# Root of the lead tiles by logarithm and exponential on ScalarE, first weight columns between the x tiles, parameter transposes behind the first tile

## Chip, cores and metric

One NeuronCore of a Trainium2 chip runs the whole kernel. The metric is device time in microseconds (us) of one execution; the kernel before took 180.91 us, the median of three runs (180.74 to 181.76). The engines are named as in the profile: PE is TensorE (PEld its weight loads), DVE is VectorE, ACT is ScalarE, POOL is GpSimd, and SP is SyncE, whose queue issues nearly all transfers.

## What is computed

The input x has 2048 tokens of 512 values. A layer normalization without weights feeds two branches, which are added to x: a diagonal state-space model with complex states (512 states, run over the 2048 tokens), and a gated feed-forward network with 1376 hidden columns.

```python
xn = (x - mean(x)) / sqrt(var(x) + 1e-5)             # over the 512 values of a token
dt = exp(log_dt); Lam_bar = exp(dt * (Lambda_re + 1j * Lambda_im))
Bu = xn @ (((Lam_bar - 1) / Lam)[:, None] * B).T     # complex
h[t] = Lam_bar * h[t - 1] + Bu[t]                    # the scan over tokens
y_A = 2 * real(h @ C.T) + xn * Dskip
y_B = (gelu(xn @ w_gate) * (xn @ w_up)) @ w_down
out = x + y_A + y_B
```

Inputs, weights and output are bf16.

## The kernel before

**Tiling.** The 2048 tokens are 16 tiles of 128, in four blocks of four tiles. For each block TensorE makes `Bu` (L671), the gate and up projections in 11 slices of up to 128 hidden columns (`gu_mm`, L728), and the down projection with the output of the state-space model added into the same PSUM bank (L802, L813). VectorE rotates and scans the states (`CHAIN`), multiplies gelu by up and evicts the output; ScalarE evicts PSUM (L680, L736, L738), applies gelu, and normalizes blocks 2 and 3.

**How the order is made.** The kernel records operations with the buffers that they read and write, and a planner with assumed durations (`Sched`) orders them. TensorE and SP keep the order of the program text. On VectorE, ScalarE and GpSimd the planner chooses, except that operations handed to `S.pin(...)` stand first, in exactly that order. `emit` (L241) then writes each operation with the semaphore waits ahead of it. An engine does its queue strictly in order, so an operation that waits holds up whatever is queued behind it. Where an activation needs a function that isn't in the table that ScalarE holds, the build puts an `ACT_TABLE_LOAD` directly in front of the activation, behind any wait that stands as an instruction of its own. Before has four of them: ahead of the first exponential (L609), the first gelu (L838), the sine (L622) and the next gelu (L838).

**The lead.** This is the stretch until TensorE begins `BU(0)` at L671, and all edits lie in it. The four tiles of block 0 are normalized one at a time so that TensorE can start early. For lead tile tt:

- `stats` (L522): VectorE takes mean and variance (L524, L525).
- `rsqrt` (L543): GpSimd adds epsilon (L544) and raises to the power -0.5 (L545).
- `center` (L537): VectorE subtracts the mean and multiplies by the root (L540). `LN_lead` (L547) pins the order on VectorE: the statistics of two tiles, centring 0, statistics 2, centring 1, statistics 3, centring 2, centring 3.
- `TR_lead` (L555): TensorE transposes the tile in four matmuls (L562) into a PSUM bank, and ScalarE copies it into `XNT` (L565, "evT").
- `lead_mm` (L833): TensorE multiplies the transposed tile by two slices each of gate and up, 8 matmuls of 128 columns for a pair of slices (L728). The program text orders them tile by tile, with the transposes between.

Ahead of and between these stand matmuls on zeros (`warm_pe`, L825), whose results nobody reads.

**The parameters.** Three vectors of 512 (log_dt, Lambda_re, Lambda_im) come as 4x128 and are turned by three small transposes on TensorE (`TR_par`, L572). ScalarE makes `exp_dt` (L609), four `exp_a` (L611) and two copies (L614, L615) from them, and VectorE the angles (L616 to L621) and the tables of sine and cosine (L626 to L630, ScalarE L632 and L633).

**SP's queue.** It issues, in this order: x tiles 0 to 3, the first 256 columns of gate and of up (`ld_gu(0)`), two transposing loads of B, then further columns and x tiles. ScalarE's queue issues the three parameter loads.

Of the kernel before, what the change touches and what calls it, by code (L numbers as in the profile page):

```python
# [10 lines left out]
ACTF = mybir.ActivationFunctionType  # L11
BF16, F32, I32 = dt.bfloat16, dt.float32, dt.int32
# [297 lines left out]
EPS_LN = 1.0e-5  # L310
# [13 lines left out]
def d_act(n, ptr=0): return 100.0 + 0.833 * n + 90.0 * ptr  # L324


def build(nc, ins, out):
    with ExitStack() as es:
        E = es.enter_context
        S = Sched(nc, es)  # L330
        ARENA_BYTES = 207 * 1024
        arena_t = E(nc.sbuf_tensor("arena", [128, ARENA_BYTES // 2], BF16))
        A = Arena(arena_t, ARENA_BYTES)
# [10 lines left out]
        WG = A.alloc("WG", [KD, F + 32], BF16)  # L344
        WU = A.alloc("WU", [KD, F], BF16)
        WD = A.alloc("WD", [KF, D], BF16)
        FCH = [(0, 256), (256, 640), (640, 1024), (1024, F)]
        WGc = [Buf("WGc%d" % i, "wg", i, i + 1) for i in range(len(FCH))]
        WUc = [Buf("WUc%d" % i, "wu", i, i + 1) for i in range(len(FCH))]
# [39 lines left out]
        MVt = [[A.sub(MV[b], "MV%d_%d" % (b, j), j) for j in range(4)] for b in range(NB)]  # L389

        def per_tile(name, dtype=F32):
            al = A.alloc(name, [NB, 4], dtype)
            blk = ring(al, name, NB)
            return blk, [[A.sub(blk[b], "%s%d_%d" % (name, b, j), j) for j in range(4)] for b in range(NB)]
        RQb, RQt = per_tile("RQ")
        NRQb, _ = per_tile("NRQ")
        NHALF = A.alloc("NHALF", [4], F32)
        HPI = A.alloc("HPI", [1], F32)
        DUM = A.alloc("DUM", [2], F32)
        LRE = A.alloc("LRE", [KP], BF16)  # L400
# [45 lines left out]
        def V(fn, dur, r, w, tag="", after=(), slack=0.0):  # L446
            op = S.op("vector", fn, dur, r, w, tag, after)
            op.slack = slack
            return op

        def ACT(fn, dur, r, w, tag="", after=(), slack=0.0):
            op = S.op("scalar", fn, dur, r, w, tag, after)
            op.slack = slack
            return op
        POOL = lambda fn, dur, r, w, tag="": S.op("gpsimd", fn, dur, r, w, tag)
        PE = lambda fn, dur, r, w, tag="": S.op("tensor", fn, dur, r, w, tag)

        def load(dst, src, nbytes, writes, tag, queue="sync"):
            return S.dma(lambda e: e.dma_start(dst, src), nbytes, writes=writes, tag=tag, queue=queue)  # L459

        def ld_x(t0, n, queue="sync"):
            return load(X_all.ap[:, t0:t0 + n, :], x2[128 * t0:128 * (t0 + n), :].rearrange("(j p) d -> p j d", p=128),
                        n * 128 * 1024, X[t0:t0 + n], "ld_x", queue)

        def ld_w(W, Wc, src, ci, queue="sync"):
            f0, f1 = FCH[ci]
            return load(W.ap[:, :, f0:f1], src[:, f0:f1].rearrange("(k p) f -> p k f", p=128),
                        512 * (f1 - f0) * 2, [Wc[ci]], "ld_w", queue)

        def ld_param(T_, nm, queue="sync"):  # L470
            return S.dma(lambda e: e.dma_start(T_.ap[0:KP, :], ins[nm].rearrange("(s p) -> s p", p=128)), 1024,
                         writes=[T_], tag="ld_" + nm, queue=queue, lat=2300.0)

        def ld_tr(dst, nm):
            return S.dma(lambda e: e.dma_start_transpose(dst.ap, ins[nm]), 4.0 * 1000 * 330, writes=[dst], tag="tr_" + nm,
                         issue=1900.0, lat=1000.0)

        def ld_gu(ci):
            ld_w(WG, WGc, ins["B_w_gate"], ci)
            ld_w(WU, WUc, ins["B_w_up"], ci)  # L480

        S.pin(*[ld_param(T_, nm, "scalar") for T_, nm in ((PRM[0], "A_log_dt"), (PRM[1], "A_Lambda_re"), (PRM[2], "A_Lambda_im"))])
        for tt in range(4):
            ld_x(tt, 1)
        ld_gu(0)
        ld_tr(BBT[0], "A_B_re")
        ld_tr(BBT[1], "A_B_im")
        ld_gu(1)
# [5 lines left out]
        def late_loads():  # L494
# [6 lines left out]
            ld_x(12, 4)  # L501

        POOL(lambda e: e.memset(NHALF.ap, -0.5), 100, [], [NHALF], "const")
        POOL(lambda e: e.iota(IOT.ap, [[1, 128]], base=0, channel_multiplier=-1), 300, [], [IOT], "iota")
        POOL(lambda e: e.iota(IOTJ.ap, [[1, 512]], base=0, channel_multiplier=0), 600, [], [IOTJ], "iotj")
        ZWs = [Buf("ZWa", "sb", ZW.lo, ZW.lo + 256, ZW.ap[:, 0:128]), Buf("ZWb", "sb", ZW.lo + 256, ZW.hi, ZW.ap[:, 128:512])]
        S.pin(V(lambda e: e.memset(ZWs[0].ap, 0.0), 100, [], ZWs[0:1], "zw"),
              V(lambda e: e.memset(ZWs[1].ap, 0.0), 200, [], ZWs[1:2], "zw"),
              V(lambda e: e.memset(HPI.ap, 0.5 * math.pi), D_TINY, [], [HPI], "hpi"),
              V(lambda e: e.memset(DUM.ap, 0.0), D_TINY, [], [DUM], "dum"),  # L510
# [11 lines left out]
        def stats(tt):  # L522
            b, j = divmod(tt, 4)
            return [V(lambda e: e.bn_stats(ST[tt].ap, X[tt].ap), 640, [X[tt]], [ST[tt]], "bnst", slack=4000.0),  # L524
                    V(lambda e: e.bn_aggr(MVt[b][j].ap, ST[tt].ap), 100, [ST[tt]], [MVt[b][j]], "bnag", slack=4000.0)]  # L525
# [11 lines left out]
        def center(tt):  # L537
            b, j = divmod(tt, 4)
            m = MVt[b][j]
            return V(lambda e: e.tensor_scalar(XN[tt].ap, X[tt].ap, m.ap[:, 0:1], RQt[b][j].ap, ALU.subtract, ALU.mult),  # L540
                     d_dve_ts4x(512) + 40, [X[tt], m, RQt[b][j]], [XN[tt]], "ln", slack=2500.0 if b == 1 else 0.0)

        def rsqrt(dst, var, r, n):  # L543
            POOL(lambda e: e.tensor_scalar(dst.ap, var, EPS_LN, None, ALU.add), 250, r, [dst], "eps")  # L544
            POOL(lambda e: e.tensor_tensor(dst.ap, dst.ap, NHALF.ap[:, 0:n], ALU.pow), (400 + 250 * n) * (1 if n == 1 else 2.5), [dst, NHALF], [dst], "pow")  # L545

        def LN_lead():  # L547
            st = [stats(tt) for tt in range(4)]
            ln = []
            for tt in range(4):  # L550
                rsqrt(RQt[0][tt], MVt[0][tt].ap[:, 1:2], [MVt[0][tt]], 1)
                ln.append(center(tt))
            S.pin(*st[0], *st[1], ln[0], *st[2], ln[1], *st[3], ln[2], ln[3])

        def TR_lead(tt):  # L555
            bank = 6 + tt % 2
            pt = PSH[bank][:, 0:512]

            def f(e):
                ins_ = None  # L560
                for dk in range(KD):
                    ins_ = e.transpose(pt[:, 128 * dk:128 * dk + 128], XN[tt].ap[:, 128 * dk:128 * (dk + 1)], IDN.ap)  # L562
                return ins_
            PE(f, 400, [XN[tt], IDN], [BANK[bank]], "T0")
            return ACT(lambda e: e.activation(XNT[0].ap[:, :, 128 * tt:128 * tt + 128],  # L565
                                              pt.rearrange("p (k t) -> p k t", k=KD), ACTF.Copy),
                       d_act(512), [BANK[bank]], [XNTt[tt]], "evT")
# [4 lines left out]
        def TR_par(i):  # L572
            PE(lambda e: e.transpose(PP[i], PRM[i].ap[0:KP, :], IDN.ap[0:KP, 0:KP]), 100, [PRM[i], IDN], [BANK[PPB[i]]], "Tp")
# [51 lines left out]
        def tables():  # L625
# [6 lines left out]
            a = ACT(lambda e: e.activation(SINT.ap, FR.ap, ACTF.Sin, scale=-SIN_SCALE), d_act(2048), [FR], [SINT], "sint")  # L632
            b_ = ACT(lambda e: e.activation(COST.ap, AFR.ap, ACTF.Sin, bias=HPI.ap, scale=-SIN_SCALE),  # L633
                     d_act(2048, 1), [AFR, HPI], [COST], "cost")
            return a, b_, preload("ld_gelu"), d
# [189 lines left out]
        def warm_pe(n, cols=512, bank=0):  # L825
            def f(e):
                ins_ = None
                for _ in range(n):
                    ins_ = e.matmul(PS[bank][:, 0:cols], ZWs[0].ap, ZW.ap[:, 0:cols], start=True, stop=True)
                return ins_  # L830
            PE(f, 0.7 * cols * n, ZWs[0:1] if cols <= 128 else ZWs, [BANK[bank]], "warm")

        def lead_mm(pairs, t0, t1):  # L833
            for k in pairs:
                gu_mm(0, k, 2 * k, 2 * k + 1, t0, t1)

        def preload(tag):
            return ACT(lambda e: e.activation(DUM.ap[:, 1:2], DUM.ap[:, 0:1], ACTF.Gelu_apprx_tanh), 1500, [DUM], [DUM], tag)  # L838

        LN_lead()  # L840
        warm_pe(2, 128)
        warm_pe(7)
        for i in range(3):
            TR_par(i)
        warm_pe(1)
        warm_pe(1, 128)
        exps, cps, dec, t3 = decay()
        evT = [TR_lead(0)]
        warm_pe(1, 512, 3)
        warm_pe(1, 256, 3)  # L850
        lead_mm((0,), 0, 1)
        evT.append(TR_lead(1))
        lead_mm((1,), 0, 1)
# [3 lines left out]
        lead_mm((0, 1), 2, 3)  # L857
        gelu0 = preload("ld_gelu")
        GATE["gelu"] = [gelu0]
        S.pin(*exps, *cps, *evT, gelu0)  # L860
        S.pin(*dec)
        for k in range(2):
            lead_mm((k,), 3, 4)
# [91 lines left out]
```

## Time and profile before

| | |
|---|---|
| median of three runs | 180.91 us |
| the profiled execution: its time, its span | 181.85 us, 180.1 us |
| TensorE busy | 176.1 us (98%) |
| VectorE busy | 161.3 us (90%) |
| ScalarE busy | 101.8 us (57%) |
| GpSimd busy | 12.9 us (7%) |
| L671 begins (end of the lead) | 12.80 us |

The span runs from the first to the last instruction that the profiler recorded; the execution's own time includes what lies around it. A row of the timeline gives start, duration, engine, source line, operation, what it writes and reads, and in brackets how long the engine had been idle and what released it. Busy time of an engine says little about the end; the chain of work that ended last, followed back from the last instruction, says which engine a delay would have to reach.

### The profile page before, as it was taken

The numbers are of one execution on the slowest core, as the hardware profiler recorded it, in microseconds if no ns is written. First come the engines' busy times: TensorE is split into PE (matmuls) and PEld (weight loads), VectorE is DVE, ScalarE is ACT, GpSimd is POOL, SyncE is SP. The second block draws the span as 40 slices with busy tenths as digits, with TensorE's granted clock in tenths as the row PEclk, the third lists the DMA queues.
The fourth block names the chain that finished last, engine by engine and source line by source line (L and its number), as shares of the span: only waits on it lengthen the run. The fifth ranks groups of instructions, "written<-read, shape, count | busy, mean of one in ns | idle before, by whom it ended". The sixth has DMA issues, their size and how long they took to land.

```text
span 180.1 us, 2424 instructions
## 1 busy us (share of the span) xinstructions
PE 176.1 (98%) x883; PEld 83.3 (46%) x883; DVE 161.3 (90%) x249; ACT 101.8 (57%) x194; POOL 12.9 (7%) x26
## 2 busy tenths in 40 slices
PE   7899999999999999999999999999999999999994
PEld 2594444444444444444444444444444444444463
DVE  5798979999799999989999999999989999999531
ACT  2469999899999999069667700037866620000000
POOL 3600120000003301600000000000000000000000
PEclk9999999999999999999999999999999999999999
DMA  5999803699500032123100000120000000002020
GB/s 133 226 247 350 256 2 75 150 239 221 128 0 0 4 70 46 58 82 63 33 2 0 0 0 0 49 73 0 0 0 0 4 0 0 0 29 87 4 87 29
DMA packets 25267, 12.38 MB, mean 69 GB/s; under 512 B 15432, under 2 KB 25256, under 8 KB 25256
## 3 DMA queue, kind: packets, MB, share of 16 engines
q1 hardware_dynamic: 25232, 12.23, 27.2%
q8 instruction: 7, 0.11, 0.3%
q14 instruction: 4, 0.03, 0.1%
q10 hardware_dynamic: 24, 0.00, 0.0%
HBM read 6.46 MB, written 2.10 MB: 48 GB/s over the span
## 4 chain that ended last, share of the span: by engine, by line
PE 94%; DMA 2%; SPq 1%; DVE 0%; issue 0%
PE PS L728 39%; PE PS L802 21%; PE PS L813 15%; PE PS L671 15%; DMA arena<-in_B_w_up_dram 2%; PE PS L760 2%; SPq L459 1%; PE PS L776 1%; PE PS L562 1%; DVE arena L820 0%
## 5 line engine op out<-in xcount | busy, mean ns | idle before, releaser
L728 PE MATMUL PS<-arena 128*128 128x512 bf16 (+1 forms) x368 | 71.9, 357 | 0.3 <-DMA arena<-in_B_w_up_dram 0.2
L728 PEld LDWEIGHTS PS<-arena 128*128 128x128 bf16 x368 | 34.2, 100 | 37.5 <-DMA arena<-in_B_w_gate_dram 0.8
L802 PE MATMUL PS<-arena 128*128 128x512 bf16 (+3 forms) x187 | 39.0, 366 | 0.0
L710 DVE TENSOR_TENSOR_SCAN arena<-arena 128x512 bf16<-128x512 f32 x32 | 38.6, 1253 | 0.0
L813 PE MATMUL PS<-arena 128*128 128x512 bf16 (+1 forms) x136 | 28.6, 366 | 0.0
L680 ACT ACTIVATE arena<-PS 128x512 bf16<-128x512 f32 x26 | 15.1, 598 | 24.0 <-PE PS L671 23.9
L671 PE MATMUL PS<-arena 128*128 128x512 bf16 x128 | 28.3, 379 | 0.0
L802 PEld LDWEIGHTS PS<-arena 128*128 128x128 bf16 (+1 forms) x187 | 18.3, 98 | 20.0
L736 ACT ACTIVATE arena<-PS 128x512 bf16<-128x512 f32 x40 | 23.9, 599 | 5.9 <-PE PS L728 5.2
L738 ACT ACTIVATE arena<-PS 128x512 bf16<-128x512 f32 x40 | 23.9, 598 | 5.3 <-PE PS L728 5.1
L813 PEld LDWEIGHTS PS<-arena 128*128 128x128 bf16 x136 | 13.3, 98 | 14.4
L671 PEld LDWEIGHTS PS<-arena 128*128 128x128 bf16 x128 | 12.4, 98 | 14.9
L740 DVE TENSOR_TENSOR arena<-arena 128x512 bf16<-128x512 bf16 x40 | 16.0, 417 | 2.7 <-ACT arena L738 2.5
L699 DVE TENSOR_TENSOR arena<-arena 128x4096 bf16<-128x4096 bf16 x8 | 18.3, 2287 | 0.1
L820 DVE TENSOR_TENSOR arena<-PS,arena 128x512 bf16<-128x512 f32 (+1 forms) x17 | 10.9, 653 | 8.2 <-PE PS L813 8.0
L700 DVE TENSOR_TENSOR arena<-arena 128x4096 bf16<-128x4096 bf16 x8 | 18.3, 2283 | 0.0
L790 DVE TENSOR_TENSOR arena<-arena 128x512 f32<-128x512 bf16 x16 | 10.8, 689 | 0.4
L701 DVE TENSOR_TENSOR arena<-arena 128x2048 bf16<-128x2048 bf16 x8 | 9.8, 1221 | 0.2
L545 POOL TENSOR_TENSOR arena<-arena 128x1 f32<-128x1 f32 (+1 forms) x7 | 7.1, 1009 | 0.6
L663 DVE SCALAR_TENSOR_TENSOR arena<-arena 128x512 bf16<-128x512 bf16 x8 | 5.7, 746 | 0.8 <-ACT arena L661 0.8
L789 DVE TENSOR_TENSOR arena<-arena 128x512 bf16<-128x512 bf16 x16 | 6.4, 417 | 0.0
L524 DVE BATCH_NORM_STATS2 arena<-arena 128x6 f32<-128x512 bf16 x8 | 5.2, 679 | 1.3 <-DMA arena<-in_A_x_dram 1.3
(70 smaller groups left out, 103.8 us busy)
## 6 DMA issues: line engine op xcount, KB each, us to landing
out_dram<-arena SPq DMA_DIRECT2D x15, 128.0 KB, 1.7
arena<-in_A_x_dram SPq DMA_DIRECT2D x3, 512.0 KB, 7.3
arena<-in_B_w_down_dram SPq DMA_DIRECT2D x1, 1280.0 KB, 8.1
arena<-in_B_w_gate_dram SPq DMA_DIRECT2D x2, 384.0 KB, 6.9
arena<-in_B_w_up_dram SPq DMA_DIRECT2D x2, 384.0 KB, 7.5
arena<-in_A_x_dram SPq DMA_DIRECT2D x4, 128.0 KB, 2.4
arena<-in_B_w_gate_dram SPq DMA_DIRECT2D x1, 352.0 KB, 7.1
arena<-in_B_w_up_dram SPq DMA_DIRECT2D x1, 352.0 KB, 7.0
```

What stands on the lines that cost most here:

```text
L671: ins_ = e.matmul(PS[bank][:, c0:c1], BBT[c].ap[:, dk, 128 * s:128 * (s + 1)], XNT[b].ap[:, dk, c0:c1], start=(dk == 0), stop=(dk == KD - 1))
L680: return ACT(lambda e: e.activation(ss.ap, PS[bank][:, :], ACTF.Copy), d_act(512), [BANK[bank]], [ss], "evBu", slack=1500.0)
L699: V(lambda e: e.tensor_tensor(TB.ap, ssb.ap, sin4, ALU.mult), d_dve_tt2x(4096), [ssb, SINT], [TB], tag)
L700: V(lambda e: e.tensor_tensor(TA.ap, ssb.ap, cos4, ALU.mult), d_dve_tt2x(4096), [ssb, COST], [TA], tag)
L710: V(lambda e, g=g, rb=rb, init=init: e.tensor_tensor_scan(g.ap, rb, g.ap, init, ALU.mult, ALU.add), d_dve_scan(512), [g, PA[RRr]] + ([CARc ...
L728: ins_ = e.matmul(PS[bank][0:m, c0:c1], W.ap[:, dk, 128 * ft:128 * ft + m], XNT[b].ap[:, dk, c0:c1], start=(dk == 0), stop=(dk == KD - 1))
L736: g = ACT(lambda e: e.activation(GG[kk].ap[0:m, :], PS[bg][0:m, :], ACTF.Gelu_apprx_tanh), d_act(512), [BANK[bg]], [GG[kk]], "gelu", after ...
L738: u = ACT(lambda e: e.activation(UPB[kk].ap[0:m, :], PS[bu][0:m, :], ACTF.Copy), d_act(512), [BANK[bu]], [UPB[kk]], "evU", slack=1500.0)
L740: h = V(lambda e: e.tensor_tensor(HTt[k2][ft].ap[0:m, :], GG[kk].ap[0:m, :], UPB[kk].ap[0:m, :], ALU.mult), d_dve_tt2x(512), [GG[kk], UPB[ ...
L802: ins_ = e.matmul(o_, HTt[k2][ft].ap[0:m, tok], WD.ap[0:m, ft, c0:c1], start=(ft == 0), stop=False)
L813: ins_ = e.matmul(o_, SSc[k3][s][c].ap[:, tok], CT[c][s].ap[:, c0:c1], start=False, stop=(s == KP - 1 and c == 1))
L820: V(lambda e, o_=o_, ko=ko: e.tensor_tensor(OUTB[ko].ap[:, c0:c1], o_, XD[ko].ap[:, c0:c1], ALU.add), d_dve_1x(c1 - c0), [part, XD[ko]], [ ...
```

## The change

The reciprocal root of the four lead tiles moves from GpSimd to ScalarE: `Ln` of variance plus epsilon, then `Exp` of that times -0.5. `LN_lead` returns these operations, and the pinned order of ScalarE weaves them with the copies `evT` and the parameter operations. On VectorE, the pinned order puts each tile's second statistics instruction behind the centring of the tile before it. On SP the first columns of gate and up move in between the x tiles. On TensorE the three parameter transposes move behind the transpose of tile 0, and the matmuls on zeros are regrouped. A constant `EPS` is set on GpSimd. Blocks 1 to 3 keep their root on GpSimd.

```diff
+        EPS = A.alloc("EPS", [1], F32)
...
-        for tt in range(4):
-            ld_x(tt, 1)
-        ld_gu(0)
+        ld_x(0, 1)
+        ld_x(1, 1)
+        ld_w(WG, WGc, ins["B_w_gate"], 0)
+        ld_x(2, 1)
+        ld_w(WU, WUc, ins["B_w_up"], 0)
+        ld_x(3, 1)
         ld_tr(BBT[0], "A_B_re")
...
         POOL(lambda e: e.memset(NHALF.ap, -0.5), 100, [], [NHALF], "const")
+        POOL(lambda e: e.memset(EPS.ap, EPS_LN), 100, [], [EPS], "const")
...
         def LN_lead():
             st = [stats(tt) for tt in range(4)]
-            ln = []
+            ln, rs = [], []
             for tt in range(4):
-                rsqrt(RQt[0][tt], MVt[0][tt].ap[:, 1:2], [MVt[0][tt]], 1)
+                var, r = MVt[0][tt].ap[:, 1:2], RQt[0][tt]
+                rs.append((ACT(lambda e, var=var, r=r: e.activation(r.ap, var, ACTF.Ln, bias=EPS.ap), 200, [MVt[0][tt], EPS], [r], "lnv"),
+                           ACT(lambda e, r=r: e.activation(r.ap, r.ap, ACTF.Exp, scale=-0.5), 200, [r], [r], "rsq")))
                 ln.append(center(tt))
-            S.pin(*st[0], *st[1], ln[0], *st[2], ln[1], *st[3], ln[2], ln[3])
+            S.pin(*st[0], st[1][0], ln[0], st[1][1], st[2][0], ln[1], st[2][1], st[3][0], ln[2], st[3][1], ln[3])
+            return rs
...
-        LN_lead()
+        rs = LN_lead()
         warm_pe(2, 128)
-        warm_pe(7)
+        warm_pe(8)
+        evT = [TR_lead(0)]
         for i in range(3):
             TR_par(i)
-        warm_pe(1)
-        warm_pe(1, 128)
+        warm_pe(1, 512, 3)
         exps, cps, dec, t3 = decay()
-        evT = [TR_lead(0)]
-        warm_pe(1, 512, 3)
-        warm_pe(1, 256, 3)
         lead_mm((0,), 0, 1)
...
-        S.pin(*exps, *cps, *evT, gelu0)
+        S.pin(*rs[0], *rs[1], evT[0], *rs[2], cps[1], exps[0], evT[1], *rs[3], evT[2], *exps[1:], cps[0], evT[3], gelu0)
         S.pin(*dec)
```

## The prediction

> **What bounds the kernel now.** I read the chain of work that ended last first, because it says which engine a delay has to reach in order to cost anything, then the timeline of the first 24 us, where every edit lies. From the page, and then from the chain in order of time (start us, us, what):
>
> ```profile
> PE 94%; DMA 2%; SPq 1%; DVE 0%; issue 0%
> ```
>
> ```profile
> 3.13 4.30 DMA arena<-in_B_w_up_dram
> 7.42 0.05 issue
> 7.47 0.61 PE PS L728 x4
> ...
> 8.50 0.85 PE PS L728 x8
> ...
> 9.78 1.17 PE PS L728 x16
> ...
> 11.18 1.79 PE PS L728 x32
> 12.96 6.91 PE PS L671 x32
> 19.87 13.81 PE PS L728 x64
> ```
>
> From 7.47 us to 177.6 us the chain is TensorE alone, piece against piece with no wait. So whatever delays TensorE in the lead (the four tiles before L671) delays the end by the same amount: nothing later has slack that could take it back. The reader should also take the pace from this view: 0.85/8 = 106 ns per 128-column matmul at 8.5 us, 1.17/16 = 73 ns at 9.8 us, 1.79/32 = 56 ns at 11.2 us. TensorE runs at half pace until about 10.2 us (6 at 106 and 10 at 53 ns make the 1.17), although the page's row of granted clock reads 9 throughout.
>
> The timeline (start us, us, engine, line, operation) shows how a lead tile goes through the engines:
>
> ```profile
> 1.95 1.28 ACT L609 ACT_TABLE_LOAD   x1 [1.95 <-issue]
> ...
> 3.67 0.18 DVE L525 BATCH_NORM_AGGREGATE arena<-arena 128x2 f32<-128x6 f32 x1
> ...
> 3.94 0.23 POOL L544 TENSOR_SCALAR arena<-arena 128x1 f32<-128x1 f32 x1 [2.33 <-DVE arena L525]
> 4.26 0.58 POOL L545 TENSOR_TENSOR arena<-arena 128x1 f32<-128x1 f32 x1
> ...
> 4.87 0.41 DVE L540 TENSOR_SCALAR arena<-arena 128x512 bf16<-128x512 bf16 x1 [0.22 <-POOL arena L545]
> ...
> 8.42 0.41 DVE L540 TENSOR_SCALAR arena<-arena 128x512 bf16<-128x512 bf16 x1 [0.84 <-POOL arena L545]
> ...
> 11.21 0.60 ACT L565 ACTIVATE arena<-PS 128x512 bf16<-128x512 bf16 x1 [0.80 <-PE PS L562]
> ...
> 11.83 1.28 ACT L838 ACT_TABLE_LOAD   x1
> ...
> 13.12 0.20 ACT L838 ACTIVATE arena<-arena 128x1 f32<-128x1 f32 x1
> ```
>
> The root takes 4.84 - 3.94 = 0.9 us on POOL. The last lead tile is centred by 8.83 us and copied out of PSUM by 11.81 us. A table load takes 1.28 us, starts 0.02 us after the operation before it ends (11.81 to 11.83) and is followed by its activation 0.01 us after its own end.
>
> **The root on ScalarE.** The queue of the changed program, as built, holds this on ScalarE ahead of the first gelu:
>
> ```
> load, Ln(0), load, Exp(0), load, Ln(1), load, Exp(1), evT(0),
> load, Ln(2), load, Exp(2), LIM copy, exp_dt, evT(1),
> load, Ln(3), load, Exp(3), evT(2), exp_a x4, LRE copy, evT(3), load, gelu
> ```
>
> Logarithm and exponential do not share the loaded table, so every Ln and every Exp has a load ahead of it: eight, where before had one (at 1.95 us, under the wait for the x tile). The first new one stands behind the wait for the variance of tile 0, so it can't hide there. Removed from POOL: eight instructions, 0.9 us per tile.
>
> Prices: a load 1.28 us; Ln and Exp on 128x1 0.20 us each, from the gelu row of that size at 13.12 us. I bound them by 0.15 us (the step of the four L611 exponentials: 4.75 to 5.34 us) and 0.30 us. With 0.02 and 0.01 us of gaps a pair costs 2 x (1.28 + 0.03 + 0.20) = 3.02 us. The sum on ScalarE starts at 3.94 us, when POOL saw the first variance:
>
> - Pair 0 ends at 6.96, pair 1 at 9.98 us. The copy evT(0), 0.60 us, is pinned behind Exp(1): 10.58.
> - Pair 2: 13.60. LIM copy and exp_dt 0.25 (rows of 0.17 to 0.20, overlapping), evT(1) 0.60: 14.45.
> - Pair 3: 17.47. evT(2) 0.60: 18.07. Four exp_a 0.60 (0.15 a step), LRE copy 0.05, evT(3) 0.60: 19.3 us.
>
> In before evT(3) ended at 11.81, so the last lead tile is 7.5 us late. Behind the waiting Ln and Exp stand the copies evT, and TensorE waits for each of them; DVE's centring waits for Exp, with the next statistics queued behind it. VectorE's centring of tile 3 (0.41) ends at 17.9, and the transpose of tile 3 (4 x 0.107) runs from 17.95 to 18.4, just ahead of its copy.
>
> **TensorE behind it.** After the transpose of tile 3 come 16 matmuls for tile 2, which need evT(2), and 16 for tile 3, which need evT(3). At full pace (56 ns, 0.90 us each) they end at 19.3 + 0.05 + 0.90 = 20.3, where before ended at about 12.9 us: 7.4 us late. At half pace the 32 take 3.4 us and end at 21.8: 8.9 us late, and L671 starts slow too. Which pace holds is not in the trace of before for such a gap, so I bound it. In before, work with gaps (0.97 to 7.47 us, some 1 us idle in all) never raised the pace; it rose at 10.2 us, 2.7 us into the first unbroken work. In the changed kernel TensorE is idle for most of 5 to 18 us, with bursts of at most some 2 us, so I take it as slow at 17.95 us. Fastest: the pace is full from there, 7.4 us. Slowest: it takes as long as from the first matmul in before, 9.2 us, so to 27.2, and L671 loses (27.2 - 21.8)/2 = 2.7 us: 11.6 us. I take some 4.2 us, between the 2.7 us and twice that, since the gap-free stretch is the nearest row: full pace from 22.1 us, 8.9 + (22.1 - 21.8)/2 = **9.1 us late**.
>
> The Trainium skill, "TensorE: Matmul & The Clock Gate", section "Part 1: The HAM clock gate", says that a free-running window of some 3.4 us must be busy before the clock doubles, and that an idle window halves it again. By it the pace would rise 3.4 to 6.8 us after 17.95 us and the estimate would be 8.7 to 10.4 us; the return to half pace is what no row of before shows.
>
> The same skill, "ScalarE: Activation LUTs", speaks both ways about the loads. Its section "Table sets: the hidden batching unit" says that one set holds both functions, so that ln then exp takes one load, and the queue above contradicts that. Its section "What ACT_TABLE_LOAD costs" adds some 1.38 us of drain to 1.28 us; eight loads would then be 11 us dearer, about 201 us, against the 0.02 and 0.01 us gaps of the rows here.
>
> **The weights between the x tiles.** x issues take 0.41 to 0.49 us each on SP, so gate goes from 2.65 to some 1.65 us, up from 3.13 to some 2.55; tiles 2 and 3 go back by 0.45 and 1.0 us. Up landed at 7.42 us, so now by some 6.8. In before that would be worth up to 0.43 us: the first four matmuls ran at 6.73 to 7.16 and waited 0.31 us for up. Now evT(0) ends at 10.58 us and the weights are no longer waited for: nothing. The later x tiles are first needed when VectorE is free of centring 0, at 7.4 us: nothing. The six issues together end where they did, so the transposing loads behind them keep their places.
>
> **Parameter transposes behind tile 0.** Three small matmuls (0.23 us at L573) and one warming matmul less net; TensorE waits anyway. What they feed, the small ScalarE operations, is in the sum above (0.9 us). VectorE's decay and table work, 6.5 us (8.75 to 15.30), now starts after centring 3, at 17.9, and ends at 24.4; the first eviction it does is then ready at 15.59 + 9.1 = 24.7. Hidden. Without that cover the bank would be late by a microsecond, and TensorE refills it 5 us later. The memset of EPS, 0.1 us on POOL, lies under the 1.25 us in which VectorE waits for x. ScalarE's later work (tables, first gelu evictions) moves with evT(3) by 7.5 us, less than TensorE does.
>
> **The sum.** Span 180.1 + 9.1 = 189.2 us. The profiled execution took 181.85 us beside its span of 180.1, while the median of the runs is 180.91, so I put the difference on the median: 180.9 + 9.1 = **190.0 us**.
>
> **Rivals.**
>
> 1. Eight loads, as forecast, with half pace at 17.95 us: 187.9 to 192.6 us by its bounds (7.4 less 0.4 for cheaper Ln and Exp, to 11.6). For it: the pace row, and the gaps. Chance 0.80.
> 2. Eight loads, but TensorE at full pace from 18 us: 180.9 + 7.4 = 188.3. For it: the granted-clock row reads 9 everywhere; against it, the 106 ns. Chance 0.10.
> 3. The loads cost more than 1.28 us when two follow each other. The widest stretch in the trace from a load's start to its activation is 2.59 us (1.95 to 4.54, there put down to the parameter transposes): 8 x 1.31 = 10.5 more, about 200.5. Against: 11.83 to 13.12. Chance 0.04.
> 4. Not slower: a load whose table already serves the next function costs nothing, so that one load remains. It ends at 5.22, Exp(0) at 5.65, centring 0 at 6.1, evT(0) at 7.3, and TensorE starts the lead at 7.35 instead of an effective 7.04 (7.47 less the 0.43 already done). A later tile takes 0.41 + 0.18 + 0.69 = 1.28 us on VectorE, so centring 3 ends at 9.95, ahead of its transpose's turn at 10.7. Result 180.9 + 0.3 = 181.2. ScalarE sat idle 3.4 us ahead of the last three copies in before, so it decides from there: up to two more loads hide, the third costs. Against: the built queue. Chance 0.06.
>
> **How the numbers follow.** The likeliest is 190.0. The range takes in rivals 1 and 2, 187.9 to 192.6. A difference within 0.5% is about what a measurement of this kernel can't tell from none; rivals 1 to 3 are slower, 0.94; rival 4 gives 0.04 for the same and 0.02 for faster, should the earlier weights bring their 0.43 us and the pace rise sooner.
>
> **What would show it.** Eight loads of 1.28 us between 3.9 and 17.3 us on ScalarE; evT(3) ending near 19.3; centring waiting for ScalarE some 1.5 to 3 us per tile; the last lead matmuls at 106 ns, and L671 starting near 21.8 and taking a little over 6.91 us; from there the same 168 us as before. I am wrong if fewer loads stand in the trace, if loads run while ScalarE waits, or if the lead matmuls of tile 3 take 56 ns.

## The result, and the profile after

The changed kernel takes 190.85 us, the median of six runs (190.48 to 191.65), beside 180.8 us for the kernel before in the same comparison (179.91 to 181.76, six runs). The ratio is 1.056, with a 95% interval of 1.0522 to 1.0598. The profiled execution took 190.94 us, its span is 189.1 us.

In the new page, the row of granted clock and the shares of the chain that ended last:

```profile
PEclk9855699999999999999999999999999999999999
...
PE 89%; ACT 7%; DMA 1%; DVE 1%; issue 1%; DVEq 0%; ACTq 0%
```

ScalarE, absent from the chain of before, now holds 7% of it. And the clock row has a dent in slices 2 to 5, that is from some 5 to 24 us. The chain in order of time (start us, us, what) shows where:

```profile
3.93 1.28 ACT L557
...
5.53 1.28 ACT L558
...
7.05 1.28 ACT L557
...
8.65 1.28 ACT L558
...
10.65 1.28 ACT L557
...
12.26 1.28 ACT L558
...
14.39 1.28 ACT L557
...
15.99 1.28 ACT L558
...
17.60 0.42 DVE arena L545
...
18.07 0.61 PE PS L570 x4
18.68 3.36 PE PS L736 x32
...
22.09 6.85 PE PS L679 x31
```

L557 is the logarithm and L558 the exponential; pieces named after the line alone are the table loads ahead of them. There are eight, 10.2 us together, one behind the other from 3.93 to 17.27 us with only the small operations and the copies between. Then come the two lines to compare with before: the 32 last lead matmuls (L736, L728 before) take 3.36 us, 105 ns each, where they took 1.79 us. L679 (L671 before) ends at 22.09 + 6.85 = 28.94 us, where it ended at 19.87: 9.07 us late. The span is longer by 9.0 us. So the whole loss is made before L679, and nothing is added or won back later. Between the medians the loss is 10.05 us, a microsecond more: the execution of before that has the profile took 181.85 us, above its median of 180.8.

The timeline of ScalarE in the lead (start us, us, engine, line, operation):

```profile
3.93 1.28 ACT L557 ACT_TABLE_LOAD   x1 [3.93 <-DVE arena L530]
5.22 0.29 ACT L557 ACTIVATE arena<-arena 128x1 f32<-128x1 f32 x1
5.53 1.28 ACT L558 ACT_TABLE_LOAD   x1
6.83 0.20 ACT L558 ACTIVATE arena<-arena 128x1 f32<-128x1 f32 x1
7.05 1.28 ACT L557 ACT_TABLE_LOAD   x1
...
10.06 0.58 ACT L573 ACTIVATE arena<-PS 128x512 bf16<-128x512 bf16 x1
...
18.71 0.60 ACT L573 ACTIVATE arena<-PS 128x512 bf16<-128x512 bf16 x1
```

The first load waits for the variance (L530). After it ScalarE has hardly a gap: 0.01 us from a load to its activation, 0.02 us from an activation to the next load. The last copy, evT(3), ends at 19.31 us.

The stretches of TensorE (start and end us, length, busy time of each engine, granted clock, DMA share, GB/s):

```profile
8.00:18.00 10.00, 5.26 (x45) 4.27 (x44) 2.21 (x8) 9.84 (x18) 0.00 (x0) 0.51 1.10 296
18.00:22.00 4.00, 3.93 (x36) 3.90 (x38) 3.86 (x14) 3.81 (x11) 0.00 (x0) 0.52 1.05 303
22.00:26.00 4.00, 3.95 (x20) 1.79 (x19) 3.61 (x5) 3.71 (x8) 0.00 (x0) 1.00 0.02 7
```

From 8 to 18 us TensorE (first number after the length) is busy for half the time, while ScalarE (fourth) works 9.84 of 10 us. The granted clock is 0.51 there and still 0.52 from 18 to 22 us, when TensorE has no gap any more.

### The profile page after: what moved, and what is told of

Its sections match the earlier page's. It is cut to its first block, busy times and chain, and to the rows that moved or that the text cites. A ratio compares the mean times of both kernels' runs of the same rounds, so it can differ in the third digit from the quotient of the medians.

```text
span 189.1 us, 2414 instructions
## 1 busy us (share of the span) xinstructions
PE 177.3 (94%) x866; PEld 85.5 (45%) x881; DVE 161.5 (85%) x249; ACT 112.9 (60%) x209; POOL 13.4 (7%) x19
## 4 chain that ended last, share of the span: by engine, by line
PE 89%; ACT 7%; DMA 1%; DVE 1%; issue 1%; DVEq 0%; ACTq 0%
PE PS L736 36%; PE PS L810 20%; PE PS L821 15%; PE PS L679 14%; ACT L558 3%; ACT L557 3%; PE PS L768 2%; DMA arena<-in_A_x_dram 1%; PE PS L784 1%; ACT arena L557 1%; ACT arena L573 1%; ACT arena L558 0%; DVE arena L529 0%; PE PS L570 0%; DVE arena L828 0%
## 5 line engine op out<-in xcount | busy, mean ns | idle before, releaser
L736 PE MATMUL PS<-arena 128*128 128x512 bf16 (+1 forms) x361 | 73.5, 367 | 2.5 <-ACT arena L573 2.1
L736 PEld LDWEIGHTS PS<-arena 128*128 128x128 bf16 x368 | 36.5, 107 | 38.7 <-issue 2.6
L821 PE MATMUL PS<-arena 128*128 128x512 bf16 (+1 forms) x136 | 28.6, 367 | 0.0
L679 PE MATMUL PS<-arena 128*128 128x512 bf16 x124 | 27.6, 379 | 0.2
L821 PEld LDWEIGHTS PS<-arena 128*128 128x128 bf16 x136 | 13.3, 98 | 14.4
L679 PEld LDWEIGHTS PS<-arena 128*128 128x128 bf16 x128 | 12.5, 98 | 14.9
L545 DVE TENSOR_SCALAR arena<-arena 128x512 bf16<-128x512 bf16 x8 | 3.0, 411 | 10.5 <-ACT arena L558 8.0
L570 PE MATMUL PS<-arena 128*128 128x128 bf16 x16 | 2.2, 287 | 5.5 <-DVE arena L545 5.5
```

What stands on the lines that cost most here:

```text
L679: ins_ = e.matmul(PS[bank][:, c0:c1], BBT[c].ap[:, dk, 128 * s:128 * (s + 1)], XNT[b].ap[:, dk, c0:c1], start=(dk == 0), stop=(dk == KD - 1))
L736: ins_ = e.matmul(PS[bank][0:m, c0:c1], W.ap[:, dk, 128 * ft:128 * ft + m], XNT[b].ap[:, dk, c0:c1], start=(dk == 0), stop=(dk == KD - 1))
L821: ins_ = e.matmul(o_, SSc[k3][s][c].ap[:, tok], CT[c][s].ap[:, c0:c1], start=False, stop=(s == KP - 1 and c == 1))
```

## The experiments

The theory: eight table loads in a row on ScalarE hold up the lead by 7.5 us, and the half pace of the matmuls behind them adds the rest. Against it stand three others: that the new order of loads and parameter transposes does it; that the hop of each tile to ScalarE and back does it, whatever the loads cost; and that VectorE's later start is the bound.

**The root back on GpSimd.** The rest of the change is kept.

```diff
-                rs.append((ACT(... ACTF.Ln ...), ACT(... ACTF.Exp ...)))
+                rsqrt(r, var, [MVt[0][tt]], 1)
+                rs.append(())
```

> The changed kernel with the root of the four lead tiles back on GpSimd; the new order of the loads, of the parameter transposes and of VectorE is kept. Theory (eight table loads on ScalarE make the delay): no load is left in the lead but the first, so about 181 us (180 to 182), the last copy evT(3) near 12 us, L679 near 13 us. First rival (the x tiles and weights in their new order, or the parameter operations behind tile 0, make the delay): about 190 us, as in the changed kernel.

Measured: 181.21 us, ratio 1.0032 (1.0004 to 1.006). L679 begins at 12.40 us. The loss is gone, so the order of loads and transposes isn't its cause. A small rest stays, 0.3%, just clear of nothing.

**Logarithm and exponential alone.** The loads and TensorE's order are those of before; the pinned orders of ScalarE and VectorE stay as in the change.

```diff
-        ld_x(0, 1); ld_x(1, 1); ld_w(WG ...); ld_x(2, 1); ld_w(WU ...); ld_x(3, 1)
+        for tt in range(4):
+            ld_x(tt, 1)
+        ld_gu(0)
...
-        warm_pe(8)
-        evT = [TR_lead(0)]
+        warm_pe(7)
         for i in range(3):
             TR_par(i)
-        warm_pe(1, 512, 3)
+        warm_pe(1)
+        warm_pe(1, 128)
         exps, cps, dec, t3 = decay()
+        evT = [TR_lead(0)]
+        warm_pe(1, 512, 3)
+        warm_pe(1, 256, 3)
```

> The logarithm and exponential on ScalarE alone, with their pinned order on ScalarE and VectorE; the loads and the order on TensorE are as before the change. Theory: eight loads stay, about 190.8 us (190 to 192), evT(3) near 19.3 us. First rival: 181 us, since what it blames is taken back.

Measured: 190.85 us, ratio 1.0557 (1.0492 to 1.0622): the whole loss from this part alone, with nothing of the new load and transpose order. Its chain ends the lead as the changed kernel's does:

```profile
18.62 3.41 PE PS L733 x32
22.03 7.00 PE PS L676 x32
```

**One load for both functions.** The set that holds logarithm and exponential is loaded by hand, once, ahead of the wait for the variance. The build then adds no load for either.

```diff
+        share = ACT(lambda e: (e.add_instruction(mybir.InstLoadActFuncSet(..., act_func_set_id=6, ...)),
+                               e.activation(DUM.ap[:, 1:2], DUM.ap[:, 0:1], ACTF.Exp))[1], 1500, [DUM], [DUM], "ld_share")
         rs = LN_lead()
...
-        S.pin(*rs[0], ...
+        S.pin(share, *rs[0], ...
```

> The changed kernel, and ahead of everything on ScalarE a load of the table set that holds both logarithm and exponential, with one exponential of a dummy behind it, so that all eight later loads fall away. Theory: the loads alone are the cost; the load lies under the wait for x, Ln 0.29 and Exp 0.20 us take the place of GpSimd's 0.9, centring 0 begins near 4.6 us and TensorE then waits for the weights of up at 7.5 us as in before: about 180.9 us (180.0 to 181.8). Second rival (the hop of each tile from VectorE to ScalarE and back, and copies pinned behind roots, make the delay, whatever the loads cost): over 185 us.

Measured: 180.81 us, ratio 1.0007 (0.9976 to 1.0038). Its timeline:

```profile
1.95 1.28 ACT L848 ACT_TABLE_LOAD   x1 [1.95 <-DVE arena L516]
...
3.92 0.29 ACT L557 ACTIVATE arena<-arena 128x1 f32<-128x1 f32 x1 [0.47 <-DVE arena L530]
4.24 0.20 ACT L558 ACTIVATE arena<-arena 128x1 f32<-128x1 f32 x1
...
7.13 0.40 PE L736 MATMUL PS<-arena 128*128 128x128 bf16 x4 [0.49 <-DMA arena<-in_B_w_up_dram]
...
7.45 0.69 DVE L529 BATCH_NORM_STATS2 arena<-arena 128x6 f32<-128x512 bf16 x1 [1.21 <-DMA arena<-in_A_x_dram]
```

The same eight activations, the same hop and the same pinned copies cost nothing that this comparison can tell once the eight loads are out. The root is then ready at 4.44 us where GpSimd had it at 4.84, but that buys nothing: TensorE waits for the weights of up, and VectorE for x tile 3, the last of the four lead tiles. The second rival is out.

**The dose.** Ln and Exp on the first one or two lead tiles, GpSimd for the others:

```diff
+                if tt < 1:      # 2 in the second kernel
                     rs.append((ACT(... ACTF.Ln ...), ACT(... ACTF.Exp ...)))
+                else:
+                    rsqrt(r, var, [MVt[0][tt]], 1)
+                    rs.append(())
```

> The changed kernel with logarithm and exponential on lead tile 0 alone, the root of tiles 1 to 3 on GpSimd: two loads instead of eight. Theory (each pair of loads moves the lead by what it takes on ScalarE, and the pace adds to it): the first copy ends near 8.6 instead of 6.6 us, L679 begins near 14.5, about 183.2 us (182.2 to 184.5). Rival (the loads cost only where a copy is queued behind them, so tile 0 alone is free): 181.

> The changed kernel with logarithm and exponential on lead tiles 0 and 1, the root of tiles 2 and 3 on GpSimd: four loads. Theory: the first copy ends near 10.6 us as in the changed kernel, TensorE then runs without a gap at half pace until some 15 us, L679 begins near 16.9, about 185.8 us (184.5 to 187.5).

Measured: 184.81 us with one tile (ratio 1.0181, 1.0129 to 1.0232) and 186.37 us with two (1.0249, 1.0185 to 1.0313); with all four it was 190.85. Two loads already cost 1.8%, some 3.3 us, so tile 0 is not free, and each further pair adds. With one tile it is 0.3 us above the range that I gave. The first copy ends at 8.86 us (8.6 expected), and L683, which is L679 of the changed kernel, begins at 15.38 us (14.5 expected); with two tiles it begins at 17.89 (16.9 expected). With one tile TensorE also waits later, once, for a transposed tile of block 1, which the changed kernel doesn't:

```profile
PE PS L683 <- DMA arena<-arena: 0.5, 1, 0.5
```

**Full pace through the lead.** Matmuls on zeros fill TensorE's gaps, and the eight loads stay. The third parameter's transpose moves to another bank to make room.

```diff
-        warm_pe(8)
+        warm_pe(16)
...
-        warm_pe(1, 512, 3)
+        warm_pe(9, 512, 3)
...
         lead_mm((1,), 0, 1)
+        warm_pe(10, 512, 4)
         evT.append(TR_lead(2))
         lead_mm((0, 1), 1, 2)
+        warm_pe(9, 512, 4)
         evT.append(TR_lead(3))
```

> The changed kernel with matmuls on zeros in the gaps of TensorE (8 more ahead of the first transpose, 8 more behind it, 10 ahead of the third, 9 ahead of the fourth), the third parameter's transpose in the bank of the other two; the eight loads stay. Theory: the half pace of the 32 last lead matmuls costs 1.4 to 1.6 us of the delay and full pace takes it back: about 189.4 us (188.9 to 190.1), matmuls at 56 ns from 18 us on. If the pace costs nothing there: 190.8 us or, with the added matmuls in the way, more.

Measured: 191.77 us, ratio 1.0601 (1.0545 to 1.0656). A miss, and a false start: the pace did become full, with L679 beginning at 20.04 us, but the time got longer. The list of waits says where that went (engine, line, waited for: us in total, times, longest):

```profile
PE PS L679 <- DMA arena<-arena: 1.8, 1, 1.8
```

The planner counts the added matmuls, and so it put VectorE's and ScalarE's work of the next blocks in another order. In that order the transposed tiles of block 2 came late, which is 1.8 of the 2.7 us by which this run is above the next one; a wait of 0.4 us for VectorE (L821) comes on top. The chain that ended last runs through VectorE for most of the time from 17.54 to 75 us. The edit had changed two things. The second try puts the added matmuls into bank columns not yet written, with no duration in the plan, and the order on the four other engines is then that of the changed kernel, instruction for instruction:

```diff
+        def fill_pe(n, bank):          # n matmuls on zeros, columns 256 to 511
+            ...
+            PE(f, 0.0, ZWs, [bank_part(bank, 1024, 2048)], "warm")
...
         warm_pe(8)
+        fill_pe(16, 0)
...
         warm_pe(1, 512, 3)
+        fill_pe(16, 3)
...
+        fill_pe(20, 0)
         evT.append(TR_lead(2))
         lead_mm((0, 1), 1, 2)
+        fill_pe(18, 0)
         evT.append(TR_lead(3))
```

> As the run with matmuls on zeros in the gaps, but with 256 columns each into bank columns not yet written (16 ahead of the first transpose, 16 behind the parameter transposes, 20 ahead of the third transpose, 18 ahead of the fourth) and with no duration in the planner, so that the order on VectorE, ScalarE, GpSimd and SP is that of the changed kernel. Theory (the half pace of the last lead matmuls is a part of the delay, and the earlier run lost it again to another order on VectorE and ScalarE that made L679 of block 2 wait for transposed tiles): L679 begins near 20.0 us instead of 21.8 to 22.1, and about 189.2 us (188.8 to 189.9). Rival (VectorE's work, which starts at 17.9 us either way, is the next bound, whatever its order): 190.8 or more.

Measured: 189.08 us, ratio 1.0417 (1.0365 to 1.0469), an interval clear of the changed kernel's. The chain:

```profile
18.36 1.79 PE PS L736 x32
...
20.21 6.85 PE PS L679 x31
```

The 32 matmuls take 1.79 us again, as in before, and 190.85 - 189.08 = 1.8 us is what the half pace cost. The two medians come from different comparisons (by the ratios it would be 2.6 us), but the traces agree with 1.8: the span is 187.3 us instead of 189.1, and L679 ends at 27.06 instead of 28.94. VectorE started its tables at 17.82 us here too, and TensorE's list of waits names it nowhere behind the lead. So the third rival is out for the order of the changed kernel; in the order of the first try it was VectorE that the chain ran through.

**Can it be made to gain?** Three kernels with the one early load: the loads as x0, gate, x1, up, x2, x3 with six added matmuls (`fill_pe(2, 0)` ahead of and `fill_pe(4, 3)` behind the first transpose); the loads in the order of before; and that with the six matmuls.

```diff
-        ld_x(0, 1); ld_x(1, 1); ld_w(WG ...); ld_x(2, 1); ld_w(WU ...); ld_x(3, 1)
+        ld_x(0, 1); ld_w(WG ...); ld_x(1, 1); ld_w(WU ...); ld_x(2, 1); ld_x(3, 1)    # first kernel
+        for tt in range(4):                                                           # second and third
+            ld_x(tt, 1)
+        ld_gu(0)
```

> One early load of the table set that holds logarithm and exponential; the loads in the order x0, gate, x1, up, x2, x3; six more matmuls of 256 columns on zeros around the first transpose. Theory: with the table loads gone TensorE waits for the weights of up and for x tile 2; up arrives some 0.5 us sooner than at 7.1 to 7.5 us, L679 begins near 11 us, and the time is 180.0 us (179.4 to 180.8), which against 180.5 for the kernel before is at the edge of what can be told. Rival: the weights arrive no sooner since the transfers share what bandwidth there is: 180.5 to 181.

> One early load of the table set that holds logarithm and exponential, Ln and Exp on ScalarE for the four lead tiles, and the loads in the order of before (x tiles 0 to 3, then gate and up). If the weights between the x tiles cost something once the table loads are gone, because x tiles 2 and 3 arrive later and up no sooner, this is below the run with one load and the new order: VectorE waits for x only once, L679 begins near 11.4 us where the pace is full, about 180.4 us (179.9 to 181.3). If their order makes no difference: 180.8 as there.

> The same with six more matmuls of 256 columns on zeros around the first transpose, without a duration in the planner. Theory: they keep TensorE busy enough that the full pace comes no later than 7 to 8 us in every execution, while up still lands near 7.4 us: 180.2 us (179.8 to 180.8), the runs closer together than those of the kernel before (180.1 to 182.3 so far). Otherwise as without them.

Measured, in this order: 181.68 us, ratio 1.0027 (0.9997 to 1.0057); 180.9 us, 1.0023 (0.999 to 1.0056); 180.55 us, 0.9994 (0.9971 to 1.0016). None is told apart from the kernel before. In the first, up landed at 6.45 us (issued at 2.25, 4.2 us to landing) against 7.12 in the run with one load and the order of the change. But x1 came late, and centring 0 is pinned behind x1's first statistics instruction:

```profile
4.83 0.69 DVE L529 BATCH_NORM_STATS2 arena<-arena 128x6 f32<-128x512 bf16 x1 [0.99 <-DMA arena<-in_A_x_dram]
```

So L736 began at 7.86 us instead of 6.26, partly behind the four matmuls that I had added. The second gave no answer on the order of the loads. The third kept its runs within 180.1 to 180.75 where before ranged from 179.84 to 182.16 beside it, but in it, too, TensorE waits 0.33 us for up, at 7.33 us. Whether the spread of before comes from the moment at which the full pace is granted is not shown, since only one of its executions has a trace. Their mean granted clocks point that way in part: beside these experiments the seven executions of before with 0.991 took 181.98 to 182.31 us, and those with 0.999 or 1.0 at most 181.89.

## Why the prediction was right, step by step

- **Eight loads, in a row.** Right: eight of 1.28 us. The first waits for the variance at 3.93 us (3.94 said).
- **The sum on ScalarE.** Right: evT(3) ends at 19.31 us, 19.3 said. Two sizes inside it were off and cancelled, which is luck. Ln took 0.29 us instead of 0.20, so that pair 0 ended at 7.03 instead of 6.96 us; and a copy starts some 0.1 us before the small operation ahead of it has ended (10.06 against 10.15).
- **Half pace.** Right: the lead matmuls run at half pace until the clock rises just before 22 us (22.1 said). The 4.2 us from the start of gap-free work to full pace was a choice between bounds; it took some 3.8 us (18.07 to 21.8). The run with full pace prices the half pace at 1.8 us in time, where the sum had 9.1 - 7.4 = 1.7. One thing under it was different: the pace had already risen once. The four transposes of tile 0 ran at full pace, those of tile 3 at half:

```profile
7.61 0.40 PE L570 MATMUL PS<-arena 128*128 128x128 bf16 x4 [2.83 <-DVE arena L545]
...
18.07 0.61 PE L570 MATMUL PS<-arena 128*128 128x128 bf16 x4 [1.42 <-DVE arena L545]
```

The granted clock fell from 1.00 at 8.1 us to 0.50 from 8.2 us. The Trainium skill, "TensorE: Matmul & The Clock Gate", section "Part 1: The HAM clock gate", says that an idle window of some 3.4 us halves the clock again and a busy one restores it. The trace agrees on the second half: 1.00 from 22 us, some 3.8 us after the gap-free work begins. On the first it shows less idle time: the longest gap in the lead was 2.83 us, and the clock fell 0.6 us after it had ended.
- **Nothing later takes it back.** Right: 9.07 us late at the end of L679, 9.0 us in the span.
- **From the span to the time.** Here the sum is off by 0.85 us. The span came out at 189.1 us (189.2 said), but the median at 190.85 (190.0 said). The 9.1 us were worked out from an execution of before that took 181.85 us, and were then put on the median; most executions of before beside the experiments took 179.8 to 180.8 us, and none of those has a trace. In the profiled one TensorE ran at half pace to 10.2 us. The run with one early load, whose first four transposes take 0.40 us and so have full pace from 5.03 us, begins L679 at 11.71 us instead of 12.80: how soon the pace rises can make about this difference. That it did so in before is not shown.
- **VectorE hidden behind TensorE.** Right: its tables start at 17.93 us and end at 24.48, its first eviction waits 0.19 us for TensorE.
- **The weights between the x tiles.** Worth nothing in the sum, as said. But the step under it failed: I had up landing at some 6.8 us because it is issued sooner. It lands at 2.73 + 4.8 = 7.53 us, not sooner than the 3.13 + 4.3 = 7.43 us of before; gate gained instead (1.65 + 3.1 = 4.75 us, before 2.65 + 3.8 = 6.45). The views of transfers (queue, form, count, KB each, us to landing), changed kernel:

```profile
arena<-in_B_w_gate_dram SPq DMA_DIRECT2D x1, 256.0 KB, 3.1
arena<-in_B_w_up_dram SPq DMA_DIRECT2D x1, 256.0 KB, 4.8
```

- **The rival that decides on the number of loads.** It was not what happened, but its mechanism is real: where one load remains the time is that of before, 180.81 us (181.2 said, with the load behind the variance; the experiment had it ahead, so the price of one load behind the variance is not tested). The Trainium skill, "ScalarE: Activation LUTs", section "Table sets: the hidden batching unit", says that one set serves both functions. The run with the set loaded by hand bears that out, and the changed kernel's eight loads show that nothing in this build picks that set by itself. Its section "What ACT_TABLE_LOAD costs" adds some 1.38 us of drain to each load; no trace here has it, the gaps are 0.01 and 0.02 us.

What stays open: the 0.3% by which the rest of the change is slower with the root on GpSimd, and which of its parts makes it. In its trace no wait of TensorE is listed behind its first transpose (5.37 us), but the 8 lead matmuls at 8.20 us still take 0.85 us, which is half pace.

## What to carry to other kernels

Before moving a small function to ScalarE, read the built queue for table loads: two functions that alternate paid 1.28 us per function and tile here, and none of it was hidden, because ScalarE was busy for 9.84 of 10 us and the other engines waited for it. If one table has both functions, load it by hand once, ahead of the first wait. Put a forecast difference on the execution that it was read from, and say how that one lies to the median. Price a stall of TensorE with the pace at which it resumes, and in an experiment that fills the stall make sure that a planner doesn't reorder the rest.

## What the runs showed of the hardware that was not expected

- Issuing a transfer 0.4 us sooner (2.73 against 3.13 us) between others did not land it sooner (7.53 against 7.43 us). The other traces agree: up landed at 6.7 to 7.4 us in the four with the order of before, and at 7.0 to 7.7 us in the seven with the order of the change. Issuing it another 0.48 us sooner, at 2.25 us, landed it at 6.45 us in one run and delayed x1, whose statistics then waited 0.99 us.
- The granted clock fell to half in the middle of work, 0.6 us after a gap of 2.83 us had ended.
- The row of the granted clock does not show the pace early in the trace: it reads 1.00 from 0 to 4 us in the changed kernel, while matmuls of 512 columns start 0.43 us apart there. At full pace those of L679 take 0.22 us (6.85 us for 31).
- The logarithm on 128x1 with its bias read from a tile took 0.29 us for all four tiles, the exponential with a constant scale 0.20 us.
